# An imaginary part summed by TensorE instead of VectorE: the first two blocks of the last part of a frequency-domain convolution

## The chip, the cores and the metric

The kernel runs on one core of a Trainium2 chip. A core has several engines that run side by side, each with its own stream of instructions: PE (TensorE, matrix multiplication), DVE (VectorE), ACT (ScalarE), POOL (GpSimd) and SP (SyncE, which issues nearly all transfers here). PE writes to PSUM, an accumulator memory, from which DVE or ACT copy (evict) results to on-chip memory (SBUF). The metric is the device time of one execution in microseconds (us), and the time of a kernel is the median over its runs.

## What is computed

The reference mixes two branches by a gate, for 2048 positions and D = 640 channels:

```python
g = sigmoid((x * gate_w).sum(-1, keepdims=True))
a = ssm_conv(x)        # a long convolution along the positions
b = (gelu(x @ w_gate) * (x @ w_up)) @ w_down
return g * a + (1 - g) * b
```

The branch `a` builds a kernel K of 2048 taps for each channel from the parameters of a state space model, and convolves by spectra:

```python
Kf = rfft2(pad(K)); Uf = rfft2(pad(x.T))
y = irfft2(Uf * Kf)[:L]
y = y.T + x * Dskip
```

What matters below is `Uf * Kf`, a product of complex numbers: its real part is Ur Kr - Ui Ki, its imaginary part Ur Ki + Ui Kr.

## The kernel before, in words

**Tiling.** The 640 channels are cut into five parts of 128. The 2048 positions are cut into four blocks of 512, and the convolution is a small polynomial product over these blocks: spectra of the blocks of x and of K are multiplied and summed into four output blocks, numbered 0 to 3. The transforms are matrix products with cosine and sine matrices held in SBUF (`DFT`). All arrays in the change are bf16, and the sums in PSUM are fp32.

**One part, from spectrum to output.** For each part, these steps follow each other; a letter with the numbers of part and block names each in the order of work.
- `U`, `K` with their evictions `V`, `Q`: forward transforms of x and of K, on PE.
- `P` (`products`, four steps, 0 to 3): DVE multiplies spectra and sums them. Tile `Ma` holds the sums for output blocks 0 and 1, `Mb` for 2 and 3. Each has four products for each block, indexed `[block, i, k]`: `[0, 0]` is Ur Kr, `[1, 1]` Ui Ki, `[0, 1]` and `[1, 0]` the two terms of the imaginary part. `mult` (line 813) makes products, `add` (line 818) adds a tile of products `Tp` to a sum, and `join` makes two halves into one: line 821 subtracts `[1, 1]` from `[0, 0]`, and line 823 adds `[1, 0]` to `[0, 1]`. After step 1 `Ma` is complete and joined, `Mb` in steps 2 and 3.
- `I` (two blocks) and `J` (one block): `inverse`, on PE. For each block it forms a real contribution (r = 0) and an imaginary one (r = 1), for two column halves `e` and four row blocks `m`: 2 x 2 x 4 = 16 matmuls of 128 x 128 by 128 x 128 (line 869), each with a load of weights of its own, when both parts are joined. Four matmuls in a row (over `m`) add to the same 128 columns in PSUM.
- `z`, `j`: the eviction of an inverse, by ACT or DVE, as a last letter A or D says (lines 127 and 131).
- `Z` (`unfold`): for a group of parts and a block of positions, PE makes the output block from the inverse by products with `ident`, `flip` and `flipn` (line 893), adds the skip term (line 897, `diag`) and the other branch (line 899, `ob`), in two halves; each half is scaled and evicted in two pieces (lines 129 on ACT and 133 on DVE), and SP writes the block to memory (line 904).

The other branch (`u`, line 632, then `l`, `b`, `G`, `g`, and `D`, line 794) fills PE between these steps.

**Order.** The whole order of work is written out by hand in the string `ORDER`; the tile framework adds semaphores for data and buffers, and keeps each engine's instructions in a fixed order. The last line of it is the tail of the kernel: the products of the last part (4) in steps 1 to 3, its inverses `J41`, `J40`, `J43`, `J42`, and the unfolds.

**What a letter A does to a join.** The letter at the end of a `P` step goes to `products` as `eng`. It doesn't move work to ACT: with A, `join` leaves line 823 out, and `joined` records False for the blocks, and `inverse` takes both halves for the imaginary part:

```python
if eng != "A":
    tt(out=M[:, c0:c1, 0, 1], in0=M[:, c0:c1, 0, 1], in1=M[:, c0:c1, 1, 0], op=ALU.add)
...
halves_of = ((0, r),) if r == 0 or joined[part, c] else ((0, 1), (1, 0))
```

Each entry of `halves_of` is a matmul of its own inside the loop over `m`, with the same weights as the other, and adds to the same place in PSUM.

**Buffers.** PSUM holds two buffers named `cv` (inverses, transforms, most unfolds) and two named `gu` (the other branch, and the unfolds `Z21` and `Z23`). Around the change the `cv` buffers go in turn to `Z03`, `Z11`, `J41`, `J40`, `Z12`, `Z10`, `Z20`, `J43`, `J42`, `Z22`, `Z13`, so an inverse or unfold has to wait until the one two places before it has been evicted.

Of the kernel before, what the change touches and what calls it, by code (L numbers as in the profile page):

```python
# [48 lines left out]
Q32A K31 P21D z10A D12 l21 P22D b21 Z00A G20 d12A P23D Q31A l30 Z01A g20 D20 K42 U40 G21 z01A K40 P13D d20D I11 g21  # L49
V40A z11A Q40A K41 b30 G30 D21 I20 U42 D23 Q41A K33 d23D K43 d21A Q33A l31 Q43M P30D D22 d22A Z02A Q42A g30 U41 P31D  # L50
b31 D30 V41D I21 G31 V42A U43 z20D V43D d30D g31 z21A P40D D32 P32D P33D d32A I30 z30A D31 J33 j33D d31A D33 J32 d33A
Z03A P41D Z11A P42D J41 J40 j41A P43D j40A j32A Z12A Z10A Z20D J43 J42 j43D Z21D j42A Z22M Z23D Z13D
"""


# [1055 lines left out]
```

## Time and profile before

| | |
|---|---|
| three runs | 317.36, 318.61, 318.88 us, median 318.61 |
| the profiled execution | 319.25 us, of which the span of its instructions 317.1 |
| instructions | 6300 |
| HBM read, written | 30.86 MB, 18.16 MB |

The profile shows one execution. Its page has the busy time of each engine and its share of the span, and the span cut into 40 equal slices (7.9 us each) with the busy share in tenths. Other views used below: a table by stretches of time (busy time of each engine, number of instructions in brackets, granted clock of PE and the share of the transfers); the chain of waits, which goes back from the last instruction to what released each, and is shown in order of time (start, length, engine, line); and the timeline (start, length, engine, line, operation, output<-inputs, shapes; merged instructions as x and their number; in square brackets the idle time before, and what ended it). PEld is the loading of weights, which overlaps PE. Matmuls overlap each other: one lasts longer than the distance to the next.

### The profile page before, as it was taken

To read this page: it belongs to the slowest core of one execution; us is meant where nothing else is said; L and a number is where in the kernel's file an instruction comes from. 1 tells how busy PE (TensorE), PEld (TensorE's weight loads), DVE (VectorE), ACT (ScalarE), POOL (GpSimd) and SP (SyncE) were. 2 spreads that over 40 slices of the span, in tenths; PEclk is the share of its full clock that TensorE was granted. 3 is DMA by queue.
4 is the path that set the end of the run, shared out by engine and by line. 5 is a ranking of instruction groups with operands and counts; after the bars stand their busy time and mean duration, and the time that the engine had idled before them with its cause. 6 is when DMAs were issued, how large, how long until landed. Compare 5 with 4: busy or idle time off the path is not lost.

```text
span 317.1 us, 6300 instructions
## 1 busy us (share of the span) xinstructions
PE 294.0 (93%) x2463; PEld 182.0 (57%) x2463; DVE 296.2 (93%) x417; ACT 246.9 (78%) x349; POOL 14.2 (4%) x78
## 2 busy tenths in 40 slices
PE   3499999999999999999998879999999999999994
PEld 2344444444555344454476567666686887687773
DVE  4887989999998999999999999989999999999984
ACT  7979999999898999998998667927696737542750
POOL 7720000000000000000000000000000000000000
PEclk9999999999999999999999999999999999999999
DMA  7997456566628885544594699946925352900233
GB/s 214 182 257 193 168 184 207 182 194 216 182 70 178 210 276 179 150 110 128 103 270 151 118 317 236 234 116 168 244 74 165 89 151 63 265 2 0 58 95 83
DMA packets 102543, 51.40 MB, mean 162 GB/s; under 512 B 44081, under 2 KB 95730, under 8 KB 102514
## 3 DMA queue, kind: packets, MB, share of 16 engines
q1 hardware_dynamic: 102256, 50.48, 59.8%
q0 software_dynamic: 256, 0.53, 0.6%
q8 instruction: 19, 0.31, 0.4%
q14 instruction: 10, 0.08, 0.1%
q10 hardware_dynamic: 2, 0.00, 0.0%
HBM read 30.86 MB, written 18.16 MB: 155 GB/s over the span
## 4 chain that ended last, share of the span: by engine, by line
PE 47%; DVE 22%; ACT 14%; DMA 8%; issue 5%; SPq 2%; DVEq 0%; ACTq 0%
PE gu L794 15%; PE gu L632 8%; PE cv L869 6%; DVE ph L413 5%; PE cv L735 4%; PE cv L718 4%; DMA Wd<-in_B_w_down_dram 3%; ACT eA L385 2%; ACT eB L385 2%; PE cv L893 2%; DMA T<-in_A_u_dram 2%; DMA Kd<-Kraw 2%; DVE ph L421 2%; DVE eB L590 1%; DVE sB L589 1%
## 5 line engine op out<-in xcount | busy, mean ns | idle before, releaser
L632 PE MATMUL gu<-xT,W 128*128 128x512 bf16 x540 | 123.7, 383 | 2.8 <-ACT GU L127 1.7
L632 PEld LDWEIGHTS <-W 128*128 128x128 bf16 x540 | 52.3, 99 | 70.1 <-issue 12.5
L794 PE MATMUL gu<-Wd,HT 128*128 128x320 bf16 x448 | 64.4, 299 | 1.1 <-DMA Wd<-in_B_w_down_dram 1.1
L794 PEld LDWEIGHTS <-HT 128*128 128x128 bf16 x448 | 43.5, 98 | 19.2 <-issue 1.3
L429 ACT ACTIVATE T<-ph 128x1024 bf16<-128x1024 int16 (+3 forms) x40 | 46.3, 1196 | 2.6 <-DVE ph L413 1.5
L127 ACT CAST GU<-gu 128x1024 bf16<-128x1024 f32 (+1 forms) x33 | 32.2, 981 | 4.6 <-PE gu L632 3.2
L813 DVE TENSOR_TENSOR Tp<-Uf,Kf 128x6144 bf16<-128x6144 bf16 (+2 forms) x15 | 34.3, 2287 | 0.1
L778 ACT ACTIVATE HT<-HT 128x1792 bf16<-128x1792 bf16 x16 | 26.5, 1692 | 7.0 <-DMA HT<-GUd 5.5
L818 DVE TENSOR_TENSOR Mb<-Mb,Tp 128x4096 bf16<-128x4096 bf16 (+1 forms) x15 | 29.0, 1933 | 0.2
L131 DVE CAST GU<-gu 128x1024 bf16<-128x1024 f32 (+1 forms) x23 | 27.0, 1174 | 0.5 <-PE gu L632 0.5
L735 PE MATMUL cv<-KTt,DFT 128*128 128x128 bf16 x280 | 24.2, 219 | 0.6 <-ACT Uf L127 0.3
L129 ACT ACTIVATE ob<-gu,rat 128x640 bf16<-128x640 f32 x12 | 9.5, 795 | 18.3 <-PE gu L794 18.3
L385 ACT ACTIVATE eB<-a 128x256 bf16<-128x256 f32 (+2 forms) x63 | 23.3, 451 | 0.0
L735 PEld LDWEIGHTS <-DFT 128*128 128x128 bf16 x280 | 21.0, 98 | 1.2 <-issue 0.4
L718 PE MATMUL cv<-pm,DFT 128*128 128x512 bf16 x80 | 20.1, 378 | 1.3 <-DVE Kraw L133 0.6
L127 ACT CAST Uf<-cv 128x1024 bf16<-128x1024 f32 x17 | 16.9, 1019 | 5.2 <-PE cv L718 3.2
L129 ACT ACTIVATE Kf<-cv 128x512 bf16<-128x512 f32 x33 | 17.6, 597 | 3.8 <-PE cv L735 3.7
L413 DVE SCALAR_TENSOR_TENSOR ph<-b,phi 128x256 int32<-128x256 f32 (+1 forms) x63 | 19.6, 385 | 0.0
L869 PEld LDWEIGHTS <-DFT 128*128 128x128 bf16 x320 | 18.8, 98 | 1.3 <-DVE HT L133 0.3
L735 PE MATMUL cv<-KTt,ME 128*128 128x128 bf16 x120 | 18.6, 219 | 0.0
L783 DVE TENSOR_TENSOR HT<-HT,Ut 128x1792 bf16<-128x1792 bf16 x16 | 17.1, 1086 | 0.1
L385 ACT ACTIVATE eA<-a 128x256 bf16<-128x256 f32 (+2 forms) x42 | 15.2, 444 | 0.9 <-DVE a L349 0.9
(182 smaller groups left out, 455.0 us busy)
## 6 DMA issues: line engine op xcount, KB each, us to landing
GUd<-GU SPq DMA_DIRECT2D x52, 256.0 KB, 2.3
HT<-GUd SPq DMA_DIRECT2D x16, 448.0 KB, 4.7
Ut<-GUd SPq DMA_DIRECT2D x16, 448.0 KB, 4.8
W<-in_B_w_gate_dram SPq DMA_DIRECT2D x12, 320.0 KB, 3.5
W<-in_B_w_up_dram SPq DMA_DIRECT2D x12, 320.0 KB, 4.3
fo<-in_A_u_dram SPq DMA_DIRECT2D x20, 128.0 KB, 3.0
out_dram<-GU SPq DMA_DIRECT2D x8, 256.0 KB, 2.6
T<-in_A_u_dram SPq DMA_DIRECT2D x2, 640.0 KB, 7.5
```

Source lines behind the costliest of these rows:

```text
L127: nc.scalar.copy(out=dst, in_=src)
L129: nc.scalar.activation(out=dst, in_=src, func=ACT.Copy, scale=scale)
L385: table(nc.scalar.activation(out=dst, in_=src, func=ACT.Exp, scale=float(scale)))
L413: nc.vector.scalar_tensor_tensor(out=ph[:, x, :], in0=b32[:, dsl], scalar=float(A_OF[x0 + x] + MID), in1=phi[:, dsl], op0=ALU.mult, op1=AL ...
L429: table(nc.scalar.activation(out=dst, in_=phl, func=ACT.Sin, scale=-SIN_SCALE if r and x1 > NA else SIN_SCALE))
L632: nc.tensor.matmul(p[:, r], lhsT=W[:, kt, f0:f0 + 128], rhs=xT[:, kt, 512 * c:512 * (c + 1)], start=(kt == 0), stop=(kt == KT_ - 1))
L718: nc.tensor.matmul(pU[:, ri], lhsT=dmat(e, ri, m), rhs=pm[:, ri, e].rearrange("p c d -> p (c d)"), start=(e == 0), stop=(e == 1))
L735: nc.tensor.matmul(pW[:, ri, 128 * m:128 * (m + 1)], lhsT=lhs, rhs=rhs, start=(first and x == 0 and m == 0), stop=(x == len(seq) - 1), ski ...
L794: nc.tensor.matmul(pD[:, h, 0:DH], lhsT=HT[:, ft, 128 * e:128 * e + 128], rhs=Wd[ft // 7][:, ft % 7, DH * h:DH * (h + 1)], start=(ft == 0) ...
L813: tt(out=dst.rearrange("p c h r f -> p (c h) r f"), in0=U[:, c0:c1].rearrange("p c h f -> p (c h) f")[:, :, None, :].to_broadcast([128, n, ...
L818: tt(out=M, in0=M, in1=T[:, t0:t1], op=ALU.add)
L869: nc.tensor.matmul(pY[:, c % 2, 256 * r + 128 * e:256 * r + 128 * (e + 1)], lhsT=dinv(m, r, e), rhs=pst[part][c // 2][:, c % 2, h[0], h[1] ...
```

## The change

One letter of the order is changed: step 1 of the products of part 4 gets A in place of D.

```diff
-Z03A P41D Z11A P42D J41 J40 j41A P43D j40A j32A Z12A Z10A Z20D J43 J42 j43D Z21D j42A Z22M Z23D Z13D
+Z03A P41A Z11A P42D J41 J40 j41A P43D j40A j32A Z12A Z10A Z20D J43 J42 j43D Z21D j42A Z22M Z23D Z13D
```

So line 823 isn't issued for `Ma` of part 4 (one DVE add over 128 x 1024 elements), `joined` is False for its blocks 0 and 1, and `J41` and `J40` each make 24 matmuls in place of 16. The joins of `Mb` (blocks 2 and 3, steps `P42` and `P43`) and of all other parts stay as they are.

## The prediction

> **What bounds the kernel now.** I began with the page's busy time and slices, to see whether an engine is full where the change lies.
>
> ```profile
> span 317.1 us, 6300 instructions
> PE 294.0 (93%) x2463; PEld 182.0 (57%) x2463; DVE 296.2 (93%) x417; ACT 246.9 (78%) x349; POOL 14.2 (4%) x78
> PE   3499999999999999999998879999999999999994
> DVE  4887989999998999999999999989999999999984
> ```
>
> PE and DVE are both at 93%, and both are at 9 tenths or more in slices 37 and 38 (285 to 301 us), where the edit lies. A mean can't say which of the two sets the end, so the table by stretches of time comes next, cut where the last part's inverse begins and ends.
>
> ```profile
> core 0: us, PE busy (x) PEld busy (x) DVE busy (x) ACT busy (x) POOL busy (x), PEclk, DMA share, GB/s
> 294.80:298.78 3.98, 3.92 (x36) 2.51 (x34) 3.95 (x4) 3.26 (x8) 0.00 (x0) 1.00 0.00 0
> 298.78:300.60 1.82, 1.82 (x33) 1.81 (x32) 1.78 (x2) 1.43 (x3) 0.00 (x0) 1.00 0.49 135
> 300.60:304.58 3.98, 3.82 (x36) 2.46 (x33) 3.88 (x6) 3.12 (x8) 0.00 (x0) 1.00 0.24 70
> ```
>
> Both are full again, at a granted clock of 1.00: from 298.78 to 300.60 PE is busy all of the 1.82 us. So the chain of waits has to decide, read in order of time.
>
> ```profile
> 298.80 1.97 PE cv L869 x32
> 300.77 0.43 PE cv L893 x2
> ...
> 305.57 0.44 PE cv L869 x7
> ...
> 306.52 0.62 DVE HT L133 x2
> 307.19 1.07 PE cv L869 x16
> ```
>
> The chain runs through PE's 32 matmuls of J41 and J40 (line 869), then through the unfolds Z12 and Z10 (line 893), and touches DVE only at 306.52, in an eviction. No product, sum or join of DVE stands in it between 298.80 and 306.52. PE, with the evictions that return its PSUM buffers, sets the end.
>
> **What is removed: one DVE add.** The timeline shows DVE around the join of Ma, and around the last join of Mb, for which J43 waits.
>
> ```profile
> 295.46 0.69 DVE L821 TENSOR_TENSOR Ma<-Ma 128x1024 bf16<-128x1024 bf16 x1
> 296.07 0.68 DVE L823 TENSOR_TENSOR Ma<-Ma 128x1024 bf16<-128x1024 bf16 x1
> 296.67 2.28 DVE L813 TENSOR_TENSOR Tp<-Uf,Kf 128x4096 bf16<-128x4096 bf16 x1
> ...
> 304.84 0.42 DVE L823 TENSOR_TENSOR Mb<-Mb 128x512 bf16<-128x512 bf16 x1
> 305.22 0.61 DVE L133 TENSOR_SCALAR HT<-cv,g 128x128 bf16<-128x128 f32 x2
> ```
>
> The second row, 0.68 us long, goes. Records overlap a little, so what DVE gains is start to start: 296.67 - 296.07 = 0.60 us. P42 and P43 follow without a gap, so their last join ends at about 304.66 in place of 305.26. Whether that is worth anything depends on who waits; the timeline of ACT, and that of PE below it, show it.
>
> ```profile
> 297.89 1.77 ACT L129 ACTIVATE GU<-cv,g 128x256 bf16<-128x256 f32 x4 [0.19 <-PE cv L899]
> 299.87 0.59 ACT L127 CAST pm<-cv 128x512 bf16<-128x512 f32 x1 [0.21 <-PE cv L869]
> 300.81 0.59 ACT L127 CAST pm<-cv 128x512 bf16<-128x512 f32 x1 [0.35 <-PE cv L869]
> 301.73 1.71 ACT L129 ACTIVATE GU<-cv,g 128x256 bf16<-128x256 f32 x4 [0.34 <-PE cv L899]
> 303.69 1.71 ACT L129 ACTIVATE GU<-cv,g 128x256 bf16<-128x256 f32 x4 [0.25 <-PE cv L899]
> ```
>
> ```profile
> 298.78 1.99 PE L869 MATMUL cv<-Ma,DFT 128*128 128x128 bf16 x32
> 300.61 0.59 PE L893 MATMUL cv<-fo,ident 128*128 128x512 bf16 x2
> ...
> 301.48 0.59 PE L893 MATMUL cv<-W,ident 128*128 128x512 bf16 x2
> ...
> 304.58 0.38 PE L893 MATMUL cv<-pm,ident 128*128 128x256 bf16 x2
> ...
> 304.96 0.22 PE L899 MATMUL cv<-ob,ident 128*128 128x128 bf16 x1
> ...
> 305.45 0.55 PE L869 MATMUL cv<-Mb,DFT 128*128 128x128 bf16 x7
> ```
>
> First waiter: J41 reads Ma, complete at 296.07 + 0.68 = 296.75, yet its first matmul is at 298.78. What came last is its PSUM buffer: ACT's four evictions of Z03 and Z11 begin at 297.89, and the two of Z03 are over halfway, at about 298.77. J41 gains nothing from an earlier Ma.
>
> Second waiter: J43. It needs the last join of Mb (305.26), a PSUM buffer that ACT frees at 303.69 + 1.71 = 305.40, and PE, which is busy with Z20 and Z21 before it. It starts at 305.45, just behind ACT. The join was 0.19 us early, so even with nothing added its 0.60 would have bought nothing here. Cost of the removal: 0, hidden by PE and ACT; without that cover it would be -0.60.
>
> **What is added: 16 matmuls and 16 weight loads on PE.** For each of two blocks, the imaginary part now takes both product halves: 2 column halves x 4 row blocks = 8 matmuls more, so 24 for a block in place of 16, 48 for the two in place of 32. In the two programs' instruction lists PE has 32 rows more at this place, DVE one fewer, and ACT, POOL and SP are the same, in the same order; no DMA or queue is passed by anything. The same kind of matmul stands by itself in J33, an inverse of the part before (first the timeline, then the line's own view: shortest, median and longest in ns):
>
> ```profile
> 289.27 1.06 PE L869 MATMUL cv<-Mb,DFT 128*128 128x128 bf16 x16
> ...
> L869 PEld LDWEIGHTS <-DFT x16: 97/98/98, 289.1 to 290.1; 128*128 128x128 bf16 x16
> L869 PE MATMUL cv<-Mb,DFT x16: 219/219/219, 289.3 to 290.1; 128*128 128x128 bf16 x16
> ```
>
> One takes 219 ns, its weight load 98, but sixteen take 1.06 us: (1.06 - 0.219) / 15 = 0.056 us from start to start, weight loads included. Sixteen more are 16 x 0.056 = 0.90 us. What isn't in the trace is a sum in which the real and imaginary halves alternate, each with the same weights loaded twice over. Its bounds: below, one load for each pair, nothing for the rest, cannot be, since every load is issued; a matmul has no shorter spacing here than 0.056, so 0.90 is the low end. Above: 16 x 0.098 = 1.57 if the added loads aren't overlapped, 16 x 0.219 = 3.50 if each matmul waits for the one before. I take 0.056: today's sums over four row blocks also write one PSUM place four times running and go at that pace.
>
> The Trainium skill ("TensorE: Matmul & The Clock Gate", section "Back-to-back issue gap") has about 81 ns for a matmul over 128 columns in a stream with a weight load for each, against the 56 ns of the row above; by it the sum would be 16 x 0.081 = 1.30 us, and the time 319.9. The row is of the same instruction in the same place, so it decides.
>
> A little comes back. 32 matmuls at 0.056 take 31 x 0.056 + 0.219 = 1.96 us, the row has 1.99: J40 stood 0.03 us for its PSUM buffer, free when ACT's evictions ended at 297.89 + 1.77 = 299.66. Afterwards J40 starts at 298.78 + 24 x 0.056 = 300.12, and that wait is gone. Added: 0.90 - 0.03 = 0.87 us.
>
> **Where it goes.** Is there slack behind it? J40's last matmul is issued at about 301.41, and Z12 starts near 301.48 in place of 300.61. Its buffer (freed by the copy at 299.87, now at about 300.32, over at 300.91) is not the limit. The copy of J40 moves from 300.81 to 301.68 and frees Z10's buffer at 302.27; Z10 stood ready at 301.48 and now at 302.35, with 0.08 us to spare as before. Z12's second half waits for two ACT evictions of its first (301.73 + 0.85 = 302.58), those waited for PE; Z20 (304.58) waits for the next two (303.69 + 0.86 = 304.55). Each of these waits hangs on the PE work ahead of it, so it moves as a whole: Z20 to 305.45, J43 to 306.32. The eviction of Z20 at 305.22 came 0.04 us behind its matmuls (304.96 + 0.22); it moves with them, and DVE, free 0.60 earlier, idles in front of it for about 0.6 + 0.87 = 1.5 us. That is where the saving goes. From there the chain alternates between PE and evictions, and nothing in it begins earlier. The output writes are the same and as far apart.
>
> **Sum.** 0 (DVE) + 0.90 - 0.03 = +0.87 us on the profiled execution: span 317.1 to 318.0, its own time 319.25 to 320.1. That execution stood 0.64 above the median of the three runs, 318.61; on the median the forecast is 318.61 + 0.87 = 319.5, which is 0.27% slower. About 0.5%, 1.6 us, is what a measurement of this kernel can tell from no change (its three runs lie 1.5 us apart), so this counts as within.
>
> **Rivals.**
>
> *Weight loads show (slower by over 0.5%).* Place: J41's and J40's imaginary sums. If a second load of the same weights waits until the pair's first matmul has let go of the array, each added matmul costs 0.098 and up: 318.61 + 1.57 = 320.2, at worst 318.61 + 3.50 = 322.1. It decides from a spacing of about 0.10 us, where 16 matmuls reach 1.6 us. For it: in 298.78 to 300.60 loads fill 1.81 of 1.82 us, so there is no room for a slower one. Against it: sixteen loads of 98 ns fit in J33's 1.06 us, so they already overlap each other.
>
> *Weight loads show in part (a little slower still).* The same place, with half of a load exposed: midway between the two rows, (0.056 + 0.098) / 2 = 0.077, sixteen cost 1.23 us, the time is 318.61 + 1.23 - 0.03 = 319.8. The same rows speak for it and against it. It is what the Trainium skill's 81 ns, cited above, would come to.
>
> *DVE is the bound (faster).* From 294.80 to 304.58 DVE is busy 3.95 + 1.78 + 3.88 = 9.61 of 9.78 us; if J43 were held by DVE's chain alone, and PE could take the 16 matmuls into its waits, the end would come 0.60 earlier, 318.0. Against it: PE is busy 3.92 + 1.82 + 3.82 = 9.56 us of the same stretch, 0.22 idle, which can't hold 0.90, and the join isn't in the chain. The Trainium skill ("Perfetto Trace Analysis", section "Identifying the Most-Contended Engine") would judge TensorE by its weight loads, not by matmul time; here they are busy 2.51, 1.81 and 2.46 us, which leaves room on both sides of the inverse but none in it.
>
> *It is swallowed.* If the evictions that Z12, Z10 and Z20 wait for were late for a reason of their own, the 0.87 would shorten those waits, and the time stay 318.6. Against it: ACT's rows at 301.73 and 303.69 each name PE as what ended their idle time. That the edit does nothing is the same number, but the lists show the 16 matmuls.
>
> **Chances.** Forecast 0.64; weight loads show 0.14, in part 0.10; swallowed 0.06; DVE the bound 0.06. Runs scatter by some 0.7 us on either side, which carries 0.05 of the forecast and 0.03 of the loads shown in part over +1.6 us, and 0.04 of the last two below -1.6: slower 0.22, same 0.74, faster 0.04. The range goes from DVE's gain (318.0) to a little beyond the exposed loads (320.2 and scatter: 320.8).
>
> **What would show it.** Right: line 869 on Ma as a group of 48 in 47 x 0.056 + 0.219 = 2.85 us; Z12 about 2.7 us after J41's start in place of 1.83; DVE idle some 1.5 us before Z20's eviction; J43 released by PE or ACT. Wrong: the 48 take over 3.5 us (loads show), or J43 starts less than 7.0 us after J41 (6.67 before, 7.54 forecast), which would mean that the tail had slack.

## The result, and the profile after

| | before | changed |
|---|---|---|
| median | 317.75 us (16 runs, 316.68 to 318.88) | 318.84 us (16 runs, 317.61 to 320.71) |
| ratio | 1 | 1.0032, 95% interval 1.0018 to 1.0046 |
| the profiled execution | 319.25 us, span 317.1 | 317.61 us, span 315.5 |

The changed kernel is 0.32% slower by the ratio, 1.0 us (0.6 to 1.5 by the interval; the two medians lie 1.09 apart), where 0.87 was forecast. That is less than the 0.5% below which the prediction counts a change as none.

The profiled execution of the changed kernel is the *shorter* one. This has to be read with care: J41 starts at 298.78 us in the one and at 296.27 in the other, though both programs are the same up to P41, so 2.5 us of difference lie ahead of the change and are scatter between executions. What the change does has to be read from an event ahead of it to one behind it. I take the first matmul of J41 and the start of the last eviction, and call the time between the two **the tail**. First the last row of DVE's timeline in the kernel before:

```profile
312.62 0.88 DVE L133 TENSOR_SCALAR GU<-cv,g 128x256 bf16<-128x256 f32 x2 [0.29 <-PE cv L899]
```

So the tail was 312.62 - 298.78 = 13.84 us. Now the first rows of the changed kernel's page (span and busy times), and its table by stretches, cut at the same events as before: from Z03's first weight load to J41, J41 with J40, and from Z12 to Z20.

```profile
span 315.5 us, 6331 instructions
PE 294.2 (93%) x2479; PEld 182.7 (58%) x2479; DVE 295.1 (94%) x416; ACT 246.9 (78%) x349; POOL 14.4 (5%) x78
```

```profile
core 0: us, PE busy (x) PEld busy (x) DVE busy (x) ACT busy (x) POOL busy (x), PEclk, DMA share, GB/s
292.29:296.27 3.98, 3.92 (x37) 2.50 (x35) 3.91 (x4) 3.26 (x8) 0.00 (x0) 1.00 0.00 0
296.27:298.94 2.67, 2.67 (x49) 2.67 (x48) 2.64 (x4) 1.43 (x3) 0.00 (x0) 1.00 0.68 185
298.94:302.92 3.98, 3.82 (x37) 2.46 (x33) 3.12 (x5) 3.12 (x8) 0.00 (x0) 1.00 0.03 8
```

The page is of no help: the busy shares are the same to a point. The stretches tell it: the first and the third are as long as before to 0.01 us, and the second has grown from 1.82 to 2.67 us, with PE busy all of it. In the third, DVE fell from 3.88 to 3.12 us. The chain of waits says which of the two counts:

```profile
296.29 2.82 PE cv L869 x48
299.11 0.43 PE cv L893 x2
...
303.91 0.44 PE cv L869 x7
...
304.86 0.62 DVE HT L133 x2
305.53 1.07 PE cv L869 x16
```

It is the chain of before, step by step, with a group of 48 in place of 32. The timelines of DVE, of PE and of ACT:

```profile
292.93 0.69 DVE L821 TENSOR_TENSOR Ma<-Ma 128x1024 bf16<-128x1024 bf16 x1
293.54 2.28 DVE L813 TENSOR_TENSOR Tp<-Uf,Kf 128x4096 bf16<-128x4096 bf16 x1
...
301.71 0.42 DVE L823 TENSOR_TENSOR Mb<-Mb 128x512 bf16<-128x512 bf16 x1
303.56 0.61 DVE L133 TENSOR_SCALAR HT<-cv,g 128x128 bf16<-128x128 f32 x2 [1.43 <-PE cv L899]
...
310.95 0.88 DVE L133 TENSOR_SCALAR GU<-cv,g 128x256 bf16<-128x256 f32 x2 [0.29 <-PE cv L899]
```

```profile
296.27 2.84 PE L869 MATMUL cv<-Ma,DFT 128*128 128x128 bf16 x48
298.94 0.59 PE L893 MATMUL cv<-fo,ident 128*128 128x512 bf16 x2
...
303.79 0.55 PE L869 MATMUL cv<-Mb,DFT 128*128 128x128 bf16 x7
```

```profile
297.81 0.59 ACT L127 CAST pm<-cv 128x512 bf16<-128x512 f32 x1 [0.66 <-PE cv L869]
299.14 0.59 ACT L127 CAST pm<-cv 128x512 bf16<-128x512 f32 x1 [0.75 <-PE cv L869]
```

The add of line 823 on Ma is gone, and the product of P42 follows line 821 after 0.61 us. The time that DVE saves is found again as 1.43 us of idle time ahead of Z20's eviction, where there was none. ACT too has only longer waits for PE (0.66 and 0.75, before 0.21 and 0.35). The tail is 310.95 - 296.27 = 14.68 us, 0.84 longer.

### The profile page after: what moved, and what is told of

Read it like the earlier page. It is cut to its first block, busy times and chain, and to the rows that moved or that the text cites. A ratio compares the mean times of both kernels' runs of the same rounds, so it can differ in the third digit from the quotient of the medians.

```text
span 315.5 us, 6331 instructions
## 1 busy us (share of the span) xinstructions
PE 294.2 (93%) x2479; PEld 182.7 (58%) x2479; DVE 295.1 (94%) x416; ACT 246.9 (78%) x349; POOL 14.4 (5%) x78
## 4 chain that ended last, share of the span: by engine, by line
PE 43%; DVE 27%; ACT 19%; issue 5%; DMA 4%; SPq 0%; ACTq 0%; DVEq 0%
PE gu L794 12%; PE gu L632 11%; PE cv L869 5%; PE cv L735 4%; DMA Ut<-GUd 4%; DVE Tp L813 4%; DVE ph L413 4%; ACT T L429 3%; ACT eB L385 3%; PE cv L718 3%; ACT GU L127 3%; DVE HT L783 3%; ACT eA L385 2%; PE cv L893 2%; DVE Mb L818 2%
## 5 line engine op out<-in xcount | busy, mean ns | idle before, releaser
L735 PEld LDWEIGHTS <-DFT 128*128 128x128 bf16 x280 | 21.0, 98 | 1.2 <-issue 0.4
L869 PEld LDWEIGHTS <-DFT 128*128 128x128 bf16 x336 | 19.6, 98 | 1.4 <-DVE HT L133 0.3
```

Of the source, the lines that this page charges most:

```text
L735: nc.tensor.matmul(pW[:, ri, 128 * m:128 * (m + 1)], lhsT=lhs, rhs=rhs, start=(first and x == 0 and m == 0), stop=(x == len(seq) - 1), ski ...
L869: nc.tensor.matmul(pY[:, c % 2, 256 * r + 128 * e:256 * r + 128 * (e + 1)], lhsT=dinv(m, r, e), rhs=pst[part][c // 2][:, c % 2, h[0], h[1] ...
```

## The experiments

Each was timed against the kernel before on the same chip as it, though not all on one chip. The tail is read from the profile, from the start of line 869's group on Ma to the start of the last eviction; among the runs with 16 added matmuls and an unchanged order it is the same to 0.01 us, where the whole time scatters by more than 1, so the small effects are read from the tail and the ratio says whether the whole time goes along.

| run | matmuls added in the tail | DVE's work before Z20 | tail, us | DVE idle before Z20, us | ratio (95%) |
|---|---|---|---|---|---|
| before | 0 | - | 13.84 | 0 | 1 |
| changed | 16 | -0.60 | 14.68 | 1.43 | 1.0032 (1.0018 to 1.0046) |
| add left out | 0 | -0.60 | 13.83 | 0.56 | 0.999 (0.9969 to 1.0011) |
| add kept | 16 | 0 | 14.69 | 0.81 | 1.0027 (1.0000 to 1.0055) |
| before, more DVE | 0 | +1.26 | 15.03 | 0 | 1.0035 (1.0014 to 1.0055) |
| changed, more DVE | 16 | +0.66 | 14.68 | 0.15 | 1.0014 (0.9990 to 1.0038) |
| matmuls doubled | 32 | -0.60 | 15.58 | 2.32 | 1.0060 (1.0034 to 1.0085) |
| two joins on PE | 24 | -0.94 | 15.19 | 1.75 | 1.0039 (1.0019 to 1.0059) |
| all joins on PE | 32 | -1.28 | 16.71 | 2.09 | 1.0106 (1.0074 to 1.0138) |
| Z20 on ACT too | 0 | - | 14.45 | - | 1.0023 (1.0003 to 1.0043) |

**The removal alone.** The kernel before, with the add left out and nothing put in its place:

```diff
-Z03A P41D Z11A P42D J41 J40
+Z03A P41A Z11A P42D J41 J40
...
-                joined[part, c + (2 if M is Mb else 0)] = eng != "A"
+                joined[part, c + (2 if M is Mb else 0)] = True
```

> The kernel before, with the add of line 823 left out for Ma of the last part, and nothing put in its place: J41 and J40 keep 16 matmuls each, so one term of the imaginary part of the last part's blocks 0 and 1 is missing from the output. Theory (PE and the evictions set the end of the tail, DVE's 0.60 us is worth nothing): the time of the kernel before, ratio 1.000; from the first matmul of J41 to the last eviction start 13.84 us as before; DVE idles about 0.6 us before the eviction of Z20. Rival (DVE's chain to J43 sets the end): 0.60 us less, ratio 0.998, and 13.24 us.

PE's timeline has 32 matmuls again, and DVE's has the gap:

```profile
297.76 1.99 PE L869 MATMUL cv<-Ma,DFT 128*128 128x128 bf16 x32
```

```profile
304.19 0.61 DVE L133 TENSOR_SCALAR HT<-cv,g 128x128 bf16<-128x128 f32 x2 [0.56 <-PE cv L899]
...
311.59 0.88 DVE L133 TENSOR_SCALAR GU<-cv,g 128x256 bf16<-128x256 f32 x2 [0.29 <-PE cv L899]
```

The tail is 311.59 - 297.76 = 13.83 us. The 0.60 us of DVE are worth 0.01: the DVE rival falls. What was saved stands as 0.56 us of idle time, ended by PE.

**The addition alone.** The changed kernel, with the add kept on DVE:

```diff
-            if eng != "A":
+            if True:
                 tt(out=M[:, c0:c1, 0, 1], in0=M[:, c0:c1, 0, 1], in1=M[:, c0:c1, 1, 0], op=ALU.add)
```

> The changed kernel with the add of line 823 kept on DVE as well: J41 and J40 take 24 matmuls each, so one term of the imaginary part of the last part's blocks 0 and 1 is counted twice in the output. Theory: the 16 matmuls are the whole cost, 16 x 0.056 = 0.9 us, so the time of the changed kernel (+0.85 over before, ratio 1.0027); from J41 to the last eviction start 14.68 us as in the changed kernel; DVE idles about 0.8 us before the eviction of Z20 in place of 1.43. Rival (part of DVE's saving is already in the changed kernel's time): up to 0.60 us more than the changed kernel, 15.3 us.

The tail is 14.69 us, that of the changed kernel; the gap of DVE shrinks from 1.43 to 0.81 by what the add takes. So the whole loss comes from the 16 matmuls, and nothing of it is paid back by DVE.

**How near DVE was.** The product of P43 made twice, in the kernel before and in the changed kernel:

```diff
-        mult(T[:, 0:4 - j], 0, 4 - j)
+        for _ in range(2 if last and j == 3 else 1): mult(T[:, 0:4 - j], 0, 4 - j)
```

> The kernel before, with the 1.22 us product of P43 (line 813, 128 x 2048) made twice, which changes no value. Theory (in the kernel before DVE came only 0.04 us ahead of Z20's eviction, so it is a second bound that lies right behind PE): nearly all of the 1.22 us is added, +1.1 to +1.25, ratio 1.0037; from J41 to the last eviction start about 15.0 us; no idle time of DVE before the eviction of Z20. Rival (DVE has slack there as it isn't in the chain): 0 to +0.3 us.

> The changed kernel, with the 1.22 us product of P43 (line 813, 128 x 2048) made twice, which changes no value. Theory (the change turned DVE's time into 1.43 us of idle time before the eviction of Z20): it fits into that gap, so nothing over the changed kernel, +0.85 over before, ratio 1.0027; from J41 to the last eviction start 14.68 us; DVE idle 0.2 us before the eviction of Z20. Rival (DVE is a bound of the tail after the change too): 0.6 to 1.2 us over the changed kernel, 15.3 to 15.9 us.

In the kernel before, J43 and the second half of Z20 now wait for DVE, on PE's timeline, and DVE's goes from the last join to Z20's eviction without a gap:

```profile
298.08 1.99 PE L869 MATMUL cv<-Ma,DFT 128*128 128x128 bf16 x32
...
305.61 0.55 PE L869 MATMUL cv<-Mb,DFT 128*128 128x128 bf16 x7 [0.74 <-DVE Mb L821]
306.37 0.27 PE L893 MATMUL cv<-pm,flip 128*128 128x256 bf16 x1 [0.21 <-DVE HT L133]
```

```profile
305.04 0.42 DVE L821 TENSOR_TENSOR Mb<-Mb 128x512 bf16<-128x512 bf16 x1
305.38 0.42 DVE L823 TENSOR_TENSOR Mb<-Mb 128x512 bf16<-128x512 bf16 x1
305.72 0.60 DVE L133 TENSOR_SCALAR HT<-cv,g 128x128 bf16<-128x128 f32 x2
```

Two things can be read here. J43 starts at 305.61, behind line 821 (305.46) and while line 823 is still at work (to 305.80): its first matmuls are those of the real part, and need only the subtraction. In the kernel before, the subtraction ended at 304.92, and J43 at 305.45 had 0.53 us to spare:

```profile
304.50 0.42 DVE L821 TENSOR_TENSOR Mb<-Mb 128x512 bf16<-128x512 bf16 x1
```

And Z20's eviction, with no idle time before it, follows the start of the join by 0.34 us (305.72 - 305.38); in the kernel before it followed by 0.38 (305.22 - 304.84), so there DVE had been ready 0.04 us ahead of PE. Counted from J41, Z20's eviction comes 1.20 us later than before, and the tail grows by 1.19 us to 15.03. In the changed kernel the same product fits into the gap, as DVE's timeline shows, and the tail stays at 14.68:

```profile
299.07 2.48 DVE L813 TENSOR_TENSOR Tp<-Uf,Kf 128x2048 bf16<-128x2048 bf16 x2
...
303.19 0.42 DVE L823 TENSOR_TENSOR Mb<-Mb 128x512 bf16<-128x512 bf16 x1
303.76 0.61 DVE L133 TENSOR_SCALAR HT<-cv,g 128x128 bf16<-128x128 f32 x2
```

So in the kernel before, DVE and PE arrive at Z20's eviction within 0.04 us of each other: more DVE work is paid nearly in full (1.19 of 1.26 us), less of it brings nothing. With the extra product in both, the edit is a gain in the tail, 14.68 against 15.03. (The whole times, 1.0014 and 1.0035, have intervals that overlap, so the gain isn't shown in them.)

**Twice the matmuls, same order.** The changed kernel, with three terms in place of two:

```diff
-halves_of = ((0, r),) if r == 0 or joined[part, c] else ((0, 1), (1, 0))
+halves_of = ((0, r),) if r == 0 or joined[part, c] else ((0, 1), (1, 0), (1, 0))
```

(and `start` and `stop` by the position in that list). It was made after the two runs that stand below it here, and its expectation refers to the first of them.

> The changed kernel with one of the two added sets of matmuls of J41 and J40 made twice (32 in each block in place of 24), so one term of the imaginary part of the last part's blocks 0 and 1 is counted twice in the output; the order of everything else is that of the kernel before. Theory (each added matmul with its load costs 0.056 us on the path that sets the end): 0.9 us over the changed kernel, 1.75 us over before, ratio 1.0055; line 869 on Ma as a group of 64 in 63 x 0.056 + 0.219 = 3.75 us; from the first matmul of J41 to the last eviction start 15.57 us. Rival (the run with all four joins on PE was dearer than 0.056 a matmul because more matmuls in a row cost more each): 16.5 us, near the 16.7 of that run.

```profile
297.76 3.73 PE L869 MATMUL cv<-Ma,DFT 128*128 128x128 bf16 x64
```

From 32 to 48 to 64 the tail goes from 13.84 to 14.68 to 15.58. The spacing in the groups is (1.99 - 0.22) / 31 = 0.057, (2.84 - 0.22) / 47 = 0.056 and (3.73 - 0.22) / 63 = 0.056 us. The starts of the single matmuls show why the first is larger: in the kernel before, the 17th, J40's first, starts 0.099 us after the 16th, and all others follow at 0.055 or 0.056. In the groups of 48 and 64 of the changed kernel and of this run no distance is over 0.056. So J40 waited 0.043 us, and the wait is gone.

**All four joins on PE.** `P42A` and `P43A` as well as `P41A`:

> The changed kernel with A for P42 and P43 as well, so that all four blocks of the last part have their imaginary part summed by PE: 32 matmuls more than before, and three adds of DVE fewer (0.60 + 0.34 + 0.34 = 1.28 us). The framework puts some of the unfolds after Z20 into another order. Theory (DVE's time is worth nothing in the tail, each matmul 0.056): 32 x 0.056 = +1.8 us over before, ratio 1.0056; from the first matmul of J41 to the last eviction start about 15.6 us; DVE idle about 2.1 us before the eviction of Z20. Rival (DVE's time is paid back once enough of it is taken off): +0.5 us over before or less, 14.4 us.

The count was right, the price was not: 16.71 us, 1.13 more than the doubled matmuls, which are as many. The end of PE's timeline, and of DVE's, show a wait that no other run has:

```profile
312.73 0.38 PE L893 MATMUL cv<-fo,flip 128*128 128x512 bf16 x1 [1.18 <-DVE GU L133]
```

```profile
311.54 0.35 DVE L133 TENSOR_SCALAR HT<-cv,g 128x128 bf16<-128x128 f32 x1 [0.58 <-ACT HT L129]
311.81 0.87 DVE L133 TENSOR_SCALAR GU<-cv,g 128x256 bf16<-128x256 f32 x2
```

With J43 and J42 longer, the framework has put the eviction of Z13's first half behind the last one of Z22, which waits for ACT; Z13's second half waits for it on PE. So the order of another engine moved with the longer matmul groups, and the wait on PE (1.18) is about the difference (1.13).

**Two joins on PE.** `P41A` and `P42A`, where DVE's order of evictions stays:

> The changed kernel with A for P42 as well (block 2 summed by PE, 8 matmuls more in J42); DVE's evictions keep their order, but PE gets some matmuls of Z21, Z23 and Z22 in another order. Theory (0.056 for each matmul; what made the run with all four joins dearer was the order of DVE's evictions at the end, which isn't changed here): 0.45 us over the changed kernel, 1.3 us over before, ratio 1.004; from the first matmul of J41 to the last eviction start 15.1 us. Rival (PE's new order around Z21 is what was dear): 15.5 us or more.

The tail is 15.19 us, 0.51 over the changed kernel for 8 matmuls (0.45 at 0.056): PE's new order around Z21 costs 0.06 at most. The 1.1 us of the run above come with DVE's order, or with J43; the two were not parted further.

**Using the idle ACT.** `Z20M` in place of `Z20D` in the kernel before, an attempt at a faster tail:

> The kernel before, with the evictions of Z20 split between ACT and DVE (Z20M in place of Z20D); the framework moves some of PE's matmuls around J43 and Z21. Theory (the tail after Z20 goes back and forth between PE and evictions, and ACT stands idle there for 2.9 us): two evictions of 0.35 us run side by side in place of one behind the other, about 0.25 us less for each half that PE waits for, so 0.2 to 0.5 us less, ratio 0.999; from the first matmul of J41 to the last eviction start 13.35 to 13.6 us. Rival (the matmuls of J43 fill that time on PE anyway): 13.84 us as before.

The expectation was wrong: 14.45 us, 0.61 longer. The timelines of ACT, DVE and PE:

```profile
305.36 0.37 ACT L129 ACTIVATE HT<-cv,g 128x128 bf16<-128x128 f32 x1
```

```profile
305.76 0.35 DVE L133 TENSOR_SCALAR HT<-cv,g 128x128 bf16<-128x128 f32 x1 [0.47 <-ACT HT L129]
307.08 0.69 DVE L131 CAST pm<-cv 128x512 bf16<-128x512 f32 x1 [0.97 <-PE cv L869]
```

```profile
307.82 1.05 PE L869 MATMUL cv<-Mb,DFT 128*128 128x128 bf16 x16 [0.73 <-DVE pm L131]
```

DVE's half of the pair starts when ACT's has ended (305.36 + 0.37 = 305.73), so the two don't run side by side; and J42 now waits 0.73 us for the eviction of J43. What each of the two costs was not parted. No version here that computes the whole output beats the kernel before.

## Why the prediction was right

- **What bounds the tail.** PE with the evictions that return its buffers: shown, from both sides. Less DVE work is worth 0.01 us of tail (add left out), and more PE work is paid, 0.84 us for the first 16 matmuls and 0.90 for the next. What the prediction didn't say is how narrow this was: DVE is a second bound that came 0.04 us ahead of PE (before, more DVE).
- **The removal, 0.** Shown by the run that makes the removal alone. The gap that was to appear in front of Z20's eviction, about 1.5 us, is 1.43. One reading in it was off and cost nothing: J43's start doesn't need the last join of Mb but only line 821 before it, as the run with more DVE shows. So J43 had 0.53 us to spare on DVE's side, not 0.19; the place where DVE comes close is Z20's eviction.
- **The addition, 16 x 0.056 = 0.90.** The group of 48 was to take 2.85 us and took 2.84; from 48 to 64 the tail grew by 0.90. The bounds above it (0.098 and 0.219 for each) are excluded, and with them both rivals in which weight loads show. The Trainium skill ("TensorE: Matmul & The Clock Gate", section "Back-to-back issue gap") has about 81 ns for such a pair of load and matmul; the trace doesn't agree here, with 56 ns over 64 of them in a row.
- **J40's wait, -0.03.** Right in kind and a little larger: 0.043 us by the starts of the matmuls, and gone in the changed kernel. The spacing without it is 0.0557, so the sum is 16 x 0.0557 - 0.043 = 0.85, which is what the tail shows (0.84).
- **No slack behind it.** Z12 came 2.67 us after J41's start (2.7 forecast), J43 7.52 us after it (7.54), and the tail grew by 0.84 (0.87). The rival in which waits swallow the matmuls falls.
- **The whole.** 1.0032 with 1.0018 to 1.0046 holds the forecast of 0.27%. The tail alone, 0.84 us, is 0.26%; the rest of the 1.0 us is inside the interval. The time itself came out 0.66 below the forecast (318.84 against 319.5), and that is the starting point: the median of the three runs, 318.61, stood 0.86 above that of the sixteen, 317.75. The range had room for it, since it allowed some 0.7 us for scatter; so that the time lay in the range says little for the mechanism, and the step from one kernel to the other says more.

The Trainium skill ("Perfetto Trace Analysis", section "Identifying the Most-Contended Engine") would have the engine of highest occupancy relieved first, with TensorE judged by the share of its peak arithmetic that it reaches and by its weight loads. By the weight loads that would have been DVE: from 294.80 to 304.58 it is busy 9.61 of 9.78 us, and the loads take 2.51 + 1.81 + 2.46 = 6.78. The runs don't bear this out for this stretch: 0.60 us less on DVE was worth 0.01, and 16 more matmuls on PE cost 0.84.

## What to carry to other kernels

Two engines that are full in the same stretch aren't both worth relieving: find the point at which they meet (here an eviction), and read which of them arrives last and by how much. Here, moving work from the one that arrives first, even by 0.04 us, to the one that arrives last cost what was added and gained nothing; the same move pays once the other has got more to do, as the runs with the extra product show in the tail. And a change of under half a per cent is read from an event ahead of the edit to one behind it, since the profiled execution as a whole can even have the wrong sign.

## What the runs showed that was not expected

- Splitting a pair of evictions between ACT and DVE didn't halve it: DVE's waited for ACT's (0.47 us idle in Z20's first pair), and the tail grew by 0.61 us.
- With longer groups in J43 and J42, DVE's evictions at the very end came in another order, and the run cost 1.13 us beyond its matmuls, more than 16 of them cost themselves (0.90).
